# Float64 weights converted in five instructions on two engines, with the state loads split by batch

## The chip, the cores and the metric

The kernel runs on one NeuronCore of a Trainium2 chip. The metric is the device time of one execution in microseconds. The core has a matrix engine (TensorE, PE in the profile; its weight loads are PEld), a vector engine (VectorE, DVE), an engine for activation functions (ScalarE, ACT), GpSimd (POOL), which here only builds the identity matrix, and SyncE (SP), which issues the DMAs. Each engine works through its own instructions in order; they wait for each other through semaphores.

## The reference

x has 8 batches, 8 heads, 512 rows and 64 columns; state has 32 rows in place of the 512. An attention runs in both directions between them, and both results go through a two-layer block with the activation h * erf(softplus(h)):

```python
scores = scale * np.matmul(x, state.transpose(0, 1, 3, 2))
a = np.exp(scores - scores.max(-1, keepdims=True)); a /= a.sum(-1, keepdims=True) + 1e-09
xread = np.matmul(a, state)
scores2 = scale * np.matmul(state, x.transpose(0, 1, 3, 2))
a2 = np.exp(scores2 - scores2.max(-1, keepdims=True)); a2 /= a2.sum(-1, keepdims=True) + 1e-09
sread = np.matmul(a2, x)
x = concat([xread, sread], axis=2) as (B*(S+Ns), H*D)     # 4352 x 512
h = x @ w_in                                              # w_in 512 x 2048
g = h * erf(np.maximum(h, 0.0) + np.log1p(np.exp(-np.abs(h))))
out = g @ w_out                                           # w_out 2048 x 512
```

The two weights are the product of a float32 array and a float64 scalar and arrive as float64. Everything else is float32.

## The kernel before

**Chunks and units.** The output is made in nine chunks: chunk b for b = 0 to 7 holds the 512 rows of x of batch b, and chunk 8 the 256 state rows of all batches together. d_ff is cut into four groups g of 512 columns. One pass (b, g) is called a unit here. In a unit `hidden` (L237) makes the group's activations, `project` (L254) multiplies them by the group's part of w_out and adds them up over g in four PSUM banks. `project` is kept back by one unit (`pending`, L303 to L311): project of unit (b, g) stands in the program behind hidden of the next unit. After the last group `store` writes the chunk out.

**Mixed weights.** For chunks 0 to 7, xread is never made. `mixed(b, g)` (L224) multiplies the batch's states, transposed in `states(b)` (L132), by the group's columns of w_in, and `hidden` multiplies the attention weights aT by that. Chunk 8 uses w_in itself with sT, the results of the states' half.

**Attention.** `attention(b)` (L139) transposes x (L145), makes the scores (L155) and copies them to sc (L159). From there go two halves. The x half transposes the scores back (L170), takes maximum, difference, exponential, sum and quotient per head (L173 to L188) and transposes the result into aT (L199, L201). The states' half takes its own maximum (L178) and exponential (L181), transposes a2 (L193, L195), multiplies by x (L212) and puts the result into sT (L219, L220). hidden(b, 0) needs aT[b]; sT is not needed before chunk 8.

**Weights.** `weight` (L81) brings in one piece of 128 x 2 x 512 float64 (1 MB) through a raw buffer and makes it float32 in seven VectorE instructions: exponent (L96, L98, L99), sign (L100), mantissa (L103, L106) and their product (L108). The raw buffer has the tag hs and the intermediate the tag s, which are also the tags of hidden's own tiles; hs has two buffers, s three. A group has two pieces of w_in and two of w_out, 16 pieces in all, and they are loaded and converted in chunk 0, unit by unit (L295 to L298).

**Order.** The framework orders each engine's instructions itself, by program order as priority and by when it reckons an instruction to be ready, and lets a tile wait for a free buffer of its tag; what is quoted below is the order it made. In the program attention(0) comes first, then per unit of chunk 0: weights_in(g), mixed(0, g), weights_out(g), in unit 0 the loads of x for batch 1 and states(1), then hidden(0, g), the pending project, mixed(1, g), and in unit 1 attention(1). All DMAs are issued by SP: x of batch 0 (L67, eight DMAs), the states of all batches (L75, eight DMAs, one a head), then the weights (L90).

Of the kernel before, what the change touches and what calls it, by code (L numbers as in the profile page):

```python
# [8 lines left out]
F32 = mybir.dt.float32  # L9
# [7 lines left out]
def kernel(  # L17
# [51 lines left out]

    load_x(0)  # L70

    st = const.tile([P, B, P], F32, name="st")
    for h in range(H):
        i, e = h // 2, h % 2
        nc.sync.dma_start(out=st[Ns * i:Ns * i + Ns, :, D * e:D * e + D],  # L75
                          in_=state[:, h].rearrange("b n d -> n b d"))

    w_in = const.tile([P, NK, d_ff], F32, name="w_in")
    w_out = const.tile([P, NF, d_model], F32, name="w_out")

    def weight(dst, src, shape):  # L81


        if src.dtype == F32:
            nc.sync.dma_start(out=dst, in_=src)
            return
        i = shape[1]
        n = shape[0] * i
        raw = act.tile([P, 2 * n], U32, name="hs")
        nc.sync.dma_start(out=raw.rearrange("p (o i) -> p o i", i=2 * i), in_=src.bitcast(U32))  # L90
# [5 lines left out]
        nc.vector.tensor_scalar(e, hi, 20, 0x7FF, op0=ALU.logical_shift_right,  # L96
                                op1=ALU.bitwise_and)
        nc.vector.tensor_scalar(e, e, -896.0, 0.0, op0=ALU.add, op1=ALU.max)  # L98
        nc.vector.tensor_scalar(e, e, 255.0, 8388608.0, op0=ALU.min, op1=ALU.mult)  # L99
        nc.vector.scalar_tensor_tensor(out=e, in0=hi, scalar=0x80000000, in1=e,  # L100
                                       op0=ALU.bitwise_and, op1=ALU.bitwise_or)
# [4 lines left out]
        nc.vector.scalar_tensor_tensor(out=f, in0=lo, scalar=2.0 ** -32, in1=m,  # L106
                                       op0=ALU.mult, op1=ALU.add)
        nc.vector.scalar_tensor_tensor(  # L108
            out=dst, in0=f.rearrange("p (o i) -> p o i", i=i), scalar=2.0 ** -20,
            in1=e.bitcast(F32).rearrange("p (o i) -> p o i", i=i), op0=ALU.mult, op1=ALU.mult)  # L110
# [3 lines left out]
    def weights_in(g):  # L114
        fs = slice(gw * g, gw * g + gw)
        for k in range(0, NK, 2):
            weight(w_in[:, k:k + 2, fs],
                   moe_w_in[P * k:P * k + 2 * P, fs].rearrange("(k p) f -> p k f", p=P),
                   (2, gw))

    def weights_out(g):
        for t in range(GF * g, GF * g + GF, 2):
            weight(w_out[:, t:t + 2, :],
                   moe_w_out[P * t:P * t + 2 * P].rearrange("(t p) e -> p t e", p=P),
                   (2, d_model))
# [13 lines left out]
    def attention(b):  # L139
        xt = x_t.pop(b)  # L140
# [21 lines left out]
        a2 = att.tile([P, 2, S], F32, name="a2")  # L162
        a2T = att.tile([P, 2, NC, P], F32, name="a2T")
        aT[b] = keep.tile([P, 2, S], F32, name="aT")
        z2 = small.tile([P, 2], F32, name="z2")
        for e in range(2):

            s1 = ps_at.tile([P, NC * NI, Ns], F32, name="at")
            for c in range(NC):
                nc.tensor.transpose(out=s1[:, NI * c:NI * c + NI, :],  # L170
                                    in_=sc[:, e, P * c:P * c + P], identity=ident)
            m1 = small.tile([P, NC * NI], F32, name="m1")
            nc.vector.reduce_max(out=m1, in_=s1, axis=AX.X)  # L173
            nc.vector.tensor_tensor(a[:, e], s1, m1.unsqueeze(2).to_broadcast([P, NC * NI, Ns]),
                                    op=ALU.subtract)

            m2 = small.tile([P, 1], F32, name="m2")
            nc.vector.reduce_max(out=m2, in_=sc[:, e], axis=AX.X)  # L178
            nc.vector.tensor_scalar(m2, m2, -scale, None, op0=ALU.mult)
            nc.scalar.activation(out=a[:, e], in_=a[:, e], func=ACTF.Exp, scale=scale)  # L180
            nc.scalar.activation(out=a2[:, e], in_=sc[:, e], func=ACTF.Exp, bias=m2, scale=scale,  # L181
                                 accum_out=z2[:, e:e + 1])
            z1 = small.tile([P, NC * NI], F32, name="z1")
            nc.vector.reduce_sum(out=z1, in_=a[:, e], axis=AX.X)
            nc.vector.tensor_scalar(z1, z1, 1e-9, None, op0=ALU.add)
            nc.vector.reciprocal(z1, z1)
            nc.vector.tensor_tensor(a[:, e], a[:, e],
                                    z1.unsqueeze(2).to_broadcast([P, NC * NI, Ns]), op=ALU.mult)  # L188

        for e in range(2):  # L190
            ps = ps_at.tile([P, NC, P], F32, name="at")
            for c in range(NC):
                nc.tensor.transpose(out=ps[:, c, :], in_=a2[:, e, P * c:P * c + P],  # L193
                                    identity=ident)
            nc.scalar.copy(a2T[:, e], ps)  # L195
        for e in range(2):
# [5 lines left out]

        nc.vector.tensor_scalar(z2, z2, 1e-9, None, op0=ALU.add)
        nc.vector.reciprocal(z2, z2)
        sr = ps_at.tile([P, 2, D], F32, name="at")
        for e in range(2):
            for c in range(NC):
                for i in range(NI):  # L210
                    q = slice(Ns * i, Ns * i + Ns)
                    nc.tensor.matmul(out=sr[q, e, :], lhsT=a2T[:, e, c, q],  # L212
                                     rhs=xt[:, c, 2 * i + e, :],
                                     start=(c == 0), stop=(c == NC - 1))
        sn = small.tile([P, 2, D], F32, name="sn")
        for e in range(2):
            nc.vector.tensor_scalar(sn[:, e], sr[:, e], z2[:, e:e + 1], None, op0=ALU.mult)
        ps = ps_at.tile([P, NI, Ns], F32, name="at")
        nc.tensor.transpose(out=ps, in_=sn, identity=ident)  # L219
        nc.scalar.copy(sT[:, :, b, :], ps)  # L220
# [3 lines left out]
    def mixed(b, g):  # L224
# [3 lines left out]
        for i in range(NI):  # L228
            for e in range(2):
                r, q = slice(D * e, D * e + D), slice(Ns * i, Ns * i + Ns)  # L230
                nc.tensor.matmul(out=ps[e][q, :], lhsT=stT[b][r, q],  # L231
                                 rhs=w_in[r, i, gw * g:gw * g + gw], start=True, stop=True)
# [48 lines left out]
    def pairs(b, g):  # L281
# [3 lines left out]
        return [(w_in[:, k, gw * g:gw * g + gw], sT[:, k].rearrange("p b n -> p (b n)"))  # L285
# [61 lines left out]
```

## Time and profile before

| what | value |
|---|---|
| device time, median of 3 runs | 894.59 us (893.84 to 894.81) |
| device time of the profiled execution | 890.89 us |
| its span | 889.1 us |
| TensorE busy | 835.7 us (94%) |
| VectorE busy | 354.9 us (40%) |
| ScalarE busy | 351.7 us (40%) |
| mean granted TensorE clock | 0.979 |
| DMA | 35.09 MB, 39 GB/s over the span |

The span runs from the first to the last record of the core; the device time of the same execution is 1.8 us longer. The profile page divides the span into 40 slices of 22 us, with the busy share of each engine in tenths; its windows give the busy time of the engines between any two moments. A row of the timeline has the start and the length in us, the engine, the line of the kernel, the operation, the tile written and the tiles read, the shapes, the number of instructions that were merged, and in brackets the idle time before with what ended it. A row of a group ends with the busy time, the mean of one instruction in ns, and the idle time before. float32 matmuls appear as two records each; their ends are modelled, so that a busy TensorE isn't always one at full rate.

### The profile page before, as it was taken

The numbers are of one execution on the slowest core, as the hardware profiler recorded it, in microseconds if no ns is written. First come the engines' busy times: TensorE is split into PE (matmuls) and PEld (weight loads), VectorE is DVE, ScalarE is ACT, GpSimd is POOL, SyncE is SP. The second block draws the span as 40 slices with busy tenths as digits, with TensorE's granted clock in tenths as the row PEclk, the third lists the DMA queues.
The fourth block names the chain that finished last, engine by engine and source line by source line (L and its number), as shares of the span: only waits on it lengthen the run. The fifth ranks groups of instructions, "written<-read, shape, count | busy, mean of one in ns | idle before, by whom it ended". The sixth has DMA issues, their size and how long they took to land.

```text
span 889.1 us, 7809 instructions
## 1 busy us (share of the span) xinstructions
PE 835.7 (94%) x3216; PEld 378.6 (43%) x3216; DVE 354.9 (40%) x500; ACT 351.7 (40%) x460; POOL 0.7 (0%) x6
## 2 busy tenths in 40 slices
PE   3659859999999999999999999999999999999997
PEld 1314413344444444445444544444444444445664
DVE  3888998524322252226222522244222522222121
ACT  2221531535334453436343733444344534333342
POOL 0000000000000000000000000000000000000000
PEclk9579998999999999999999999999999999999999
DMA  8533254010201020102000020100010001000100
GB/s 212 142 128 109 96 141 142 1 48 0 49 0 48 0 49 0 48 0 48 1 24 24 1 48 0 48 0 1 0 48 0 2 0 39 9 0 1 47 1 24
DMA packets 45347, 35.09 MB, mean 39 GB/s; under 512 B 36865, under 2 KB 36865, under 8 KB 45313
## 3 DMA queue, kind: packets, MB, share of 16 engines
q1 hardware_dynamic: 45312, 34.61, 12.9%
q8 instruction: 25, 0.41, 0.2%
q14 instruction: 10, 0.07, 0.0%
HBM read 25.69 MB, written 8.91 MB: 39 GB/s over the span
## 4 chain that ended last, share of the span: by engine, by line
PE 83%; DVE 11%; DMA 3%; SPq 1%; ACT 1%; issue 0%; DVEq 0%
PE o L257 49%; PE h L246 26%; PE at L231 3%; DMA hs<-in_moe_w_in_dram 3%; DVE s L106 2%; DVE s L100 2%; PE at L145 1%; DVE s L96 1%; DVE s L103 1%; DVE s L98 1%; PE at L212 1%; PE at L155 1%; PE at L199 1%; PE at L193 1%; DVE w_in L108 1%; DVE s L251 1%
## 5 line engine op out<-in xcount | busy, mean ns | idle before, releaser
L257 PE MATMUL o<-w_out,s 128*128 128x512 f32 x1088 | 488.8, 597 | 15.1 <-DVE s L251 15.1
L257 PEld LDWEIGHTS o<-w_out,s 128*128 128x128 f32 x1088 | 204.0, 191 | 260.9 <-issue 241.7
L246 PE MATMUL h<-aT,m 128*128 128x512 f32 x512 | 240.4, 606 | 6.5 <-DVE hs L249 6.5
L249 DVE COPY hs<-h 128x512 f32<-128x512 f32 (+1 forms) x144 | 95.0, 660 | 245.5 <-ACT s L248 245.5
L248 ACT ACTIVATE s<-h 128x512 f32<-128x512 f32 (+1 forms) x144 | 82.2, 574 | 185.3 <-PE h L246 184.9
L246 PEld LDWEIGHTS h<-aT,m 128*128 128x128 f32 x512 | 93.9, 192 | 131.2 <-issue 116.9
L251 DVE TENSOR_TENSOR s<-s,hs 128x2048 f32<-128x2048 f32 (+1 forms) x36 | 78.2, 2173 | 74.7 <-ACT s L250 74.7
L233 ACT COPY m<-at 128x512 f32<-128x512 f32 x32 | 18.7, 585 | 210.0 <-PE at L231 210.0
L234 DVE COPY m<-at 128x512 f32<-128x512 f32 x32 | 22.1, 689 | 166.4 <-PE at L231 166.4
L250 ACT ACTIVATE s<-s 128x2048 f32<-128x2048 f32 (+1 forms) x36 | 65.4, 1815 | 0.4
L248 ACT ACT_TABLE_LOAD x42 | 53.9, 1283 | 14.2 <-DVE w_out L108 13.5
L231 PE MATMUL at<-w_in,stT 64*32 64x512 f32 x512 | 43.2, 629 | 4.0 <-DVE w_in L108 3.7
L250 ACT ACT_TABLE_LOAD x36 | 46.2, 1283 | 0.6
L265 ACT COPY ot<-o 128x512 f32<-128x512 f32 x34 | 19.8, 581 | 65.1 <-PE o L257 65.1
L246 PE MATMUL h<-sT,w_in 128*128 128x256 f32 x128 | 28.9, 379 | 0.0
L246 PEld LDWEIGHTS h<-sT,w_in 128*128 128x128 f32 x128 | 24.3, 190 | 6.7 <-issue 3.8
L231 PEld LDWEIGHTS at<-w_in,stT 64*32 64x32 f32 x512 | 6.8, 106 | 33.7 <-issue 22.9
L145 PE MATMUL at<-ident,x 128*128 128x128 f32 x128 | 18.3, 292 | 2.5 <-DVE m L234 2.2
L145 PEld LDWEIGHTS at<-ident,x 128*128 128x128 f32 x128 | 16.1, 151 | 10.4 <-DVE m L234 3.1
L147 ACT COPY xT<-at 128x512 f32<-128x512 f32 x32 | 17.4, 590 | 7.3 <-PE at L145 7.3
L96 DVE TENSOR_SCALAR s<-hs 128x1024 uint32<-128x1024 uint32 x16 | 11.0, 688 | 22.7 <-DMA hs<-in_moe_w_in_dram 22.7
L106 DVE SCALAR_TENSOR_TENSOR s<-hs,s 128x1024 f32<-128x1024 uint32 x16 | 19.5, 1218 | 0.1
(47 smaller groups left out, 295.8 us busy)
## 6 DMA issues: line engine op xcount, KB each, us to landing
x<-in_x_dram SPq DMA_DIRECT2D x64, 128.0 KB, 3.0
hs<-in_moe_w_in_dram SPq DMA_DIRECT2D x8, 1024.0 KB, 5.2
hs<-in_moe_w_out_dram SPq DMA_DIRECT2D x8, 1024.0 KB, 6.0
out_dram<-ot SPq DMA_DIRECT2D x32, 256.0 KB, 2.3
st<-in_state_dram SPq DMA_DIRECT2D x8, 64.0 KB, 2.3
out_dram<-ot SPq DMA_DIRECT2D x8, 64.0 KB, 1.7
```

Source lines behind the costliest of these rows:

```text
L96: nc.vector.tensor_scalar(e, hi, 20, 0x7FF, op0=ALU.logical_shift_right, op1=ALU.bitwise_and)
L106: nc.vector.scalar_tensor_tensor(out=f, in0=lo, scalar=2.0 ** -32, in1=m, op0=ALU.mult, op1=ALU.add)
L145: nc.tensor.transpose(out=xp[:, P * c:P * c + P], in_=xt[:, c, 2 * i:2 * i + 2, :], identity=ident)
L231: nc.tensor.matmul(out=ps[e][q, :], lhsT=stT[b][r, q], rhs=w_in[r, i, gw * g:gw * g + gw], start=True, stop=True)
L234: nc.vector.tensor_copy(mg[:, 1], ps[1])
L246: nc.tensor.matmul(out=hp[:, 0:n], lhsT=lhsT[:, P * i:P * i + P], rhs=rhs, start=(k == 0), stop=(k == len(pairs) - 1))
L248: nc.scalar.activation(out=s[:, i, :], in_=hp[:, 0:n], func=ACTF.Softplus)
L249: nc.vector.tensor_copy(hs[:, i, :], hp[:, 0:n])
L250: nc.scalar.activation(out=s, in_=s, func=ACTF.Erf)
L251: nc.vector.tensor_tensor(s, s, hs, op=ALU.mult)
L257: nc.tensor.matmul(out=acc[r], lhsT=gT[:, i, P * r:P * r + P], rhs=w_out[:, GF * g + i, :], start=(g == 0 and i == 0), stop=(g == NG - 1 a ...
L265: nc.scalar.copy(ot, acc[r])
```

## The change

Four things are changed.

- **The conversion** of a piece has two ScalarE and three VectorE instructions. ScalarE scales the high word, read as float32, into the destination, and scales the low word in place; VectorE shifts the destination by three bits, adds the low word, and puts in the sign. The intermediate in the s buffers is gone. w_in pieces get a raw tag of their own with two buffers; w_out pieces stay in hs. w_in is laid out by group, so that a piece is contiguous.
- **The states** of batch 0 are loaded first, from ScalarE's queue; those of the other batches from SP in unit 1 of chunk 0, behind that unit's weights.
- **Attention 0** is split: `attention` returns its states' half as a function, which is called behind hidden(0, 0). For later batches it is called at once; m2 and the a2 exponential then stand behind the whole x half.
- **Batch 1 comes later**: its x and states in unit 1, mixed(1, 0) and mixed(1, 1) both in unit 1, attention(1) in unit 3 of chunk 0. Later chunks keep their places.

```diff
+    def load_st(queue, bs):
+        for h in range(H):
+            i, e = h // 2, h % 2
+            queue.dma_start(out=st[Ns * i:Ns * i + Ns, bs, D * e:D * e + D],
+                            in_=state[bs, h].rearrange("b n d -> n b d"))
+
+    load_st(nc.scalar, slice(0, 1))
     load_x(0)
...
-    w_in = const.tile([P, NK, d_ff], F32, name="w_in")
+    w_in = const.tile([P, NG, NK, GF * P], F32, name="w_in")
...
-        raw = act.tile([P, 2 * n], U32, name="hs")
+        raw = act.tile([P, 2 * shape[0] * i], U32, name=tag, bufs=bufs)
...
-        em = act.tile([P, 2, n], U32, name="s", bufs=3)
-        e, m = em[:, 0], em[:, 1]
-        nc.vector.tensor_scalar(e, hi, 20, 0x7FF, op0=ALU.logical_shift_right,
-                                op1=ALU.bitwise_and)
-        nc.vector.tensor_scalar(e, e, -896.0, 0.0, op0=ALU.add, op1=ALU.max)
-        nc.vector.tensor_scalar(e, e, 255.0, 8388608.0, op0=ALU.min, op1=ALU.mult)
-        nc.vector.scalar_tensor_tensor(out=e, in0=hi, scalar=0x80000000, in1=e,
+        dst = dst.rearrange("p o i -> p (o i)")
+        d = dst.bitcast(U32)
+        nc.scalar.activation(out=dst, in_=hi.bitcast(F32), func=ACTF.Copy, scale=2.0 ** -112)
+        nc.scalar.activation(out=lo, in_=lo, func=ACTF.Copy, scale=2.0 ** -29)
+        nc.vector.tensor_scalar(d, d, 3, None, op0=ALU.logical_shift_left)
+        nc.vector.tensor_tensor(d, d, lo, op=ALU.add)
+        nc.vector.scalar_tensor_tensor(out=d, in0=hi, scalar=0x80000000, in1=d,
                                        op0=ALU.bitwise_and, op1=ALU.bitwise_or)
-
-        nc.vector.tensor_scalar(m, hi, 0xFFFFF, 0x100000, op0=ALU.bitwise_and,
-                                op1=ALU.bitwise_or)
-        f = m.bitcast(F32)
-        nc.vector.scalar_tensor_tensor(out=f, in0=lo, scalar=2.0 ** -32, in1=m,
-                                       op0=ALU.mult, op1=ALU.add)
-        nc.vector.scalar_tensor_tensor(
-            out=dst, in0=f.rearrange("p (o i) -> p o i", i=i), scalar=2.0 ** -20,
-            in1=e.bitcast(F32).rearrange("p (o i) -> p o i", i=i), op0=ALU.mult, op1=ALU.mult)
...
-    attention(0)
+    rest = attention(0)
...
+                if g == 1:
+                    load_st(nc.sync, slice(1, B))
-            if b + 1 < B and g == 0:
+            if b + 1 < B and g == (1 if b == 0 else 0):
                 load_x(b + 1)
                 states(b + 1)
             gT = hidden(pairs(b, g), n)
+            if b == 0 and g == 0:
+                rest()
...
-            if b + 1 < B:
-                mixed(b + 1, g)
-                if g == 1:
-                    attention(b + 1)
+            if b + 1 < B and (b or g):
+                for i in [g] if b or g > 1 else [0, 1]:
+                    mixed(b + 1, i)
+                if g == (NG - 1 if b == 0 else 1):
+                    attention(b + 1)()
```

More of the change, by code (lines that the diff above doesn't have):

```diff
@@ L116, in weights_in @@
         for k in range(0, NK, 2):
-            weight(w_in[:, k:k + 2, fs],
+            weight(w_in[:, g, k:k + 2, :],
                    moe_w_in[P * k:P * k + 2 * P, fs].rearrange("(k p) f -> p k f", p=P),
-                   (2, gw))
+                   (2, gw), "raw", 2)
     def weights_out(g):
@@ L190, in attention @@
         for e in range(2):
[L191 to L196, printed above, removed]
             ps = ps_at.tile([P, S], F32, name="at")
@@ L201, in attention @@
             nc.vector.tensor_copy(aT[b][:, e], ps)
[L205 to L214, printed above, removed]
@@ L222 @@
+        return rest
     m_t = {}
```

61 lines of the change are left out of this document (37 added, 24 removed).

## The prediction

> **What bounds the kernel now.** I read the page's busy shares in 40 slices first, to see where TensorE is not the limit, then its windows by stage.
>
> ```profile
> span 889.1 us, 7809 instructions
> ...
> PE   3659859999999999999999999999999999999997
> ...
> DVE  3888998524322252226222522244222522222121
> ```
>
> ```profile
> 12.48:40.56 28.08, 17.50 (x140) 9.61 (x140) 22.86 (x41) 8.49 (x17) 0.00 (x0) 0.69 0.71 202
> 40.56:170.00 129.44, 103.55 (x422) 40.47 (x422) 113.02 (x147) 42.67 (x57) 0.00 (x0) 0.92 0.34 109
> 170.00:889.10 719.10, 714.64 (x2657) 328.51 (x2655) 219.00 (x314) 299.25 (x385) 0.00 (x0) 1.00 0.06 19
> ```
>
> The columns of a window are its length, then PE, PEld, DVE, ACT and POOL busy, the granted clock, the DMA share and GB/s. After 170 us TensorE is busy for all but the tail, at clock 1.00: nothing there is to be won or, short of a new stall, lost. Before 170 VectorE is busy 22.86 + 113.02 = 135.9 of 157.5 us, and TensorE waits and runs at 0.69 and 0.92. So the opening is bound by VectorE and by what waits for it.
>
> How much could be won follows from the work of TensorE. The chain of waits and the timeline, of one mixed and of TensorE's end, give it:
>
> ```profile
> 245.92 12.02 PE o L257 x28
> ...
> 308.08 1.24 PE at L155 x16
> ...
> 402.93 1.24 PE at L155 x16
> ```
>
> ```profile
> 119.17 1.09 PE L231 MATMUL at<-w_in,stT 64*32 64x512 f32 x16
> ```
>
> ```profile
> 836.29 3.62 PE L246 MATMUL h<-sT,w_in 128*128 128x256 f32 x16
> 839.74 1.02 PE L257 MATMUL o<-w_out,s 128*128 128x512 f32 x2
> ...
> 871.60 13.04 PE L257 MATMUL o<-w_out,s 128*128 128x512 f32 x30
> ```
>
> A matmul record at full clock takes 12.02/28 = 0.43 us, and the same place of two attentions is 402.93 - 308.08 = 94.85 us apart: one batch with everything in it (4 hidden of 16 records, 6.9 us each; 4 project of 32, 13.7 us; 4 mixed at 1.09; one attention, the rest, about 8). The last chunk is 8 x 3.45 (839.74 - 836.29) + 64 x 0.43 = 55.1. So all matmul work is 8 x 94.85 + 55.1 = 813.9 us. It starts at 12.48; the last matmul ends at 871.60 + 13.04 = 884.64, 4.5 before the end. 12.48 + 813.9 + 4.5 = 830.9: **58.2 us of the span are lost**, all before 170.
>
> Where they are lost, from the timeline of the opening:
>
> ```profile
> 0.73 5.36 SPq L67 DMA_DIRECT2D x<-in_x_dram  x8
> 6.14 4.07 SPq L75 DMA_DIRECT2D st<-in_state_dram  x8
> 10.25 0.96 SPq L90 DMA_DIRECT2D hs<-in_moe_w_in_dram  x2
> 12.48 0.45 PE L135 MATMUL at<-ident,st 128*128 128x128 f32 x1 [12.48 <-DMA st<-in_state_dram]
> 15.43 0.69 DVE L96 TENSOR_SCALAR s<-hs 128x1024 uint32<-128x1024 uint32 x1 [15.43 <-DMA hs<-in_moe_w_in_dram]
> 16.64 0.69 DVE L98 TENSOR_SCALAR s<-s 128x1024 uint32<-128x1024 uint32 x1
> 17.25 1.22 DVE L106 SCALAR_TENSOR_TENSOR s<-hs,s 128x1024 f32<-128x1024 uint32 x1
> 18.21 1.07 ACT L159 COPY sc<-at 128x512 f32<-128x512 f32 x2 [1.22 <-PE at L155]
> 18.38 0.68 DVE L99 TENSOR_SCALAR s<-s 128x1024 uint32<-128x1024 uint32 x1
> ...
> 30.03 0.69 DVE L201 COPY aT<-at 128x512 f32<-128x512 f32 x1
> ...
> 36.40 1.22 DVE L108 SCALAR_TENSOR_TENSOR w_in<-s 128x1024 f32<-128x1024 f32 x1
> ...
> 40.56 5.06 PE L246 MATMUL h<-aT,m 128*128 128x512 f32 x8
> ```
>
> The first matmul waits for the state, which SP issues behind x. attention(0) is through at 30.7, but the first w_in group only at 37.6, so the first hidden starts at 40.56. By then 9.1 us of matmul work (attention 8, mixed 1.1) are done in 28.1: **19.0 lost; the other 39.2 follow**. Who makes them wait, from the waits between 40.56 and 170:
>
> ```profile
> PE o L257 <- DVE s L251: 15.1, 3, 7.4
> ...
> ACT L248 <- DVE w_out L108: 13.5, 3, 5.0
> ...
> DVE s L96 <- DMA hs<-in_moe_w_in_dram: 7.3, 4, 2.3
> PE h L246 <- DVE hs L249: 6.5, 2, 3.3
> ```
>
> ```profile
> SPq L90 <- DVE s L100: 36.5, 7, 6.9
> SPq L90 <- DVE s L251: 23.1, 3, 10.8
> ```
>
> Each row has the sum, the times and the longest. The fourth is VectorE waiting for weights; the other three of the first group are in-order delays behind the conversion, and the s buffers that it holds. The last two, from SP's own waits, are weight loads that wait for an hs buffer, those on L251 until a whole hidden is finished.
>
> **The conversion.** Two forms are in it: the one-source operations (L96, L98, L99, L103) follow each other at 17.25 - 16.64 = 0.60 us, those with two sources (L100, L106, L108) at 18.38 - 17.25 = 1.13. Before: 4 x 0.60 + 3 x 1.13 = 5.8 a piece, 16 pieces, 93 us. After: one shift 0.60, an addition and a bitwise operation of two sources, 2 x 1.13: 2.9 a piece, 46 us. **VectorE loses 47 us** and comes to 89 in an opening whose matmul work is longer.
>
> ```profile
> L251 DVE TENSOR_TENSOR s<-s,hs 128x2048 f32<-128x2048 f32 x4 | 9.1, 2284 | 2.5 <-ACT s L250 2.5
> ```
>
> The addition of two uint32 tensors is in no row; its bounds are 0.60 (a one-source operation of that size) and 2.28 (L251, two sources and twice the size), and I take 1.13, the row of the same size with two tensor sources.
>
> ScalarE gets two operations of 128x1024 a piece. Their nearest rows in the opening are half and double:
>
> ```profile
> L248 ACT ACTIVATE s<-h 128x512 f32<-128x512 f32 x18 | 10.3, 596 | 26.9 <-PE h L246 26.9
> L250 ACT ACTIVATE s<-s 128x2048 f32<-128x2048 f32 x4 | 7.6, 1911 | 0.0
> ```
>
> Between 0.60 and 1.91, on their line, lies 0.60 + 1.31/3 = 1.03. 32 of them are **33 us on ScalarE**, which had 8.49 + 42.67 = 51.2 us of work in 157.5; bounds 32 x 0.60 = 19 and 32 x 1.91 = 61. 51 + 33 = 84 fits under the opening even if that shrinks by 58, so I cost it at nothing for the bound, but not for the latency: each piece passes two engines, about 1.0 + 1.0 + 1.1 + 1.1 = 4.2 us from landing to the end. What is queued behind a ScalarE operation that waits for a weight DMA is attention's copies and exponentials and hidden's softplus, and TensorE waits for all of them.
>
> **The loads.** Eight state issues (4.07 us) leave SP's head, so the weights go out at about 6.1 instead of 10.25. On ScalarE's queue eight issues cost between nothing and, at SP's rate, 4.07 us, before its table load; x lands later than that, so nothing. The page gives x 3.0 us from issue to landing:
>
> ```profile
> x<-in_x_dram SPq DMA_DIRECT2D x64, 128.0 KB, 3.0
> ```
>
> The last x is out at 6.1 and lands at 9.1: TensorE starts **3.4 us earlier**. The other seven batches' states (again eight issues, some 4.1 us) and x of batch 1 (5.4) go on SP, with the loads of the second and third groups behind them; these have at least 21 us of hidden and project work as cover. Without that cover they would cost their 9.5 us. The raw buffers of w_in take away the 23.1 us of loads that wait for L251, and the s buffers no longer go to the conversion (the 13.5 us of ScalarE).
>
> **The first hidden.** sc was copied 18.21 - 12.48 = 5.7 us after the first matmul, aT ready 12.5 later, at 30.7, with conversion operations between and the states' half as well. From 9.1 the same makes 27.3. VectorE by itself: the first piece lands 5.2 after its issue (15.43 - 10.25), at 11.3, so it starts around 12.8, and has ten operations of attention at 0.60, about 0.8 of small ones, two pieces (5.7) and mixed's copy: 13.1 us, to 25.9. I take **27 for the first hidden**: 13.6 earlier.
>
> **The sum.** From there: 813.9 - 9.1 and the states' half of attention 0, moved behind it. Its TensorE part is in these rows of attention 1 (the first of them twice): 2 x 0.66 + 1.10 + 0.27 = 2.7.
>
> ```profile
> 92.06 1.09 PE L145 MATMUL at<-ident,x 128*128 128x128 f32 x8 [2.21 <-DVE m L234]
> ...
> 103.57 0.66 PE L193 MATMUL at<-ident,a 128*128 128x128 f32 x4 [0.23 <-ACT a L181]
> ...
> 107.25 1.28 DVE L201 COPY aT<-at 128x512 f32<-128x512 f32 x2
> ...
> 108.47 1.10 PE L212 MATMUL at<-x,a2T 128*32 128x64 f32 x64
> ...
> 112.18 0.27 PE L219 MATMUL at<-ident,sn 128*128 128x128 f32 x1
> ```
>
> 27 + 804.8 + 2.7 + 4.5 = 839.0 without another loss. Losses that I leave in, my estimates: 3.4 because half of the first hidden still runs at the half clock (16 x 0.43 / 2; the clock was 0.69 in the window before it); 3 because VectorE owes two w_out pieces, two w_in pieces, the hidden copies and L251, some 16 us from 27, where TensorE has 13; 2 a unit for the three later units, 6; 2.6 around attention 1. That is 15: a span of **854**, 35 less. The profiled execution took 890.89 with 1.8 outside the span, so 856; the timed runs have a median of 894.59, 3.7 above the profiled one, and 894.6 - 35 gives **860**. Its own range is 850 to 867.
>
> **The rivals.** *ScalarE's order.* It is in order, and a conversion placed ahead of attention's copies waits for its DMA: VectorE already waited up to 2.3 us for the w_in loads, 7.3 in four waits. Four groups at 3 us or so more are 12 us: 872. For: two more engines' hand-overs a piece; against: ScalarE has much idle time. In sentences of its own: the Trainium skill, ScalarE: Activation LUTs, section Rules for kernel authors, has multiplications done on VectorE, not ScalarE, as up to about three times as fast there in bf16. The trace agrees in direction for float32 (0.69 against an estimated 1.03), and that trade is this rival; it decides only where ScalarE is late.
>
> *attention 1 exposed.* It moves from the second unit to the end of chunk 0. In the rows above it took 92.06 to 108.5 to aT, 16.5 us of which 5.3 (8 less 2.7) are its own matmuls; if nothing fills it, 11 us: 871. Against: project of the last two units, 27.5 us, is ready about then. In sentences of its own: the Trainium skill, TensorE: Matmul & The Clock Gate, section What's actually happening, gives half clock after an idle window of about 3.4 us; by it the exposed case would cost up to 1.7 more, an estimate from that page. The trace shows the half clock after idling (0.69 above).
>
> *Better*: the losses left in are 5, and the first hidden starts at 25: 848.
>
> *Slower than before*: the strided uint32 reads and integer writes of ScalarE are in no row. If they ran far slower than the float rows, ScalarE would bound the opening. It has 157.5 - 51.2 = 106 us free at the old length, so from 106/32 = 3.3 us each, over three times my value, the change loses; at 4 us it gives 894.6 + 32 x 0.7 = 917. Nothing in the profile points there.
>
> That the conversion path isn't taken is excluded: the loads through hs are in the trace.
>
> **Chances.** Forecast 0.50, ScalarE's order 0.20, attention exposed 0.14, better 0.09, slower 0.04, gain given back to within 0.2% (what a measurement can tell) 0.03. So faster 0.93, same 0.03, slower 0.04. 847 to 878 takes in all but the last two and the worst of the rivals.
>
> **What would show it.** Right: the first hidden before 30, VectorE some 47 us less busy, ScalarE some 33 more, the first matmul near 9, weight loads no longer waiting for L251, the distance between attentions still 94.85. Wrong: conversions of ScalarE near 2 us or more; ScalarE idle on weight DMAs ahead of softplus; TensorE idle for over 5 us between the last hidden of chunk 0 and the first of chunk 1; any TensorE gap in the later chunks.

## The result and the profile after

The changed kernel takes 855.66 us (median of 4 runs, 854.35 to 856.09) against 894.70 us for the kernel before on the same chip (4 runs, 893.84 to 896.83): a ratio of 0.9558, 95% interval 0.9538 to 0.9578. It is 39.0 us faster. The profiled execution took 856.09 us, 1.8 more than its span.

The page of the changed kernel: span, busy time of each engine, and the 40 slices (21.4 us each) of TensorE, VectorE, ScalarE and TensorE's clock.

```profile
span 854.3 us, 7812 instructions
...
PE 827.7 (97%) x3216; PEld 379.0 (44%) x3216; DVE 310.8 (36%) x436; ACT 388.9 (46%) x494; POOL 0.7 (0%) x6
...
PE   3689999999999999999999999999999999999997
...
DVE  2979524452222522262224422262224322222121
ACT  5778535563344534373344534373445434333332
...
PEclk7689999999999999999999999999999999999999
```

Before, TensorE reached nine tenths for good only in the seventh slice; now it does so in the fourth. VectorE is 44.1 us less busy (354.9 before), ScalarE 37.2 more (351.7 before). The windows of the changed kernel, cut at its first matmul, at its first hidden and at 130 us; the columns are those of the windows in the prediction:

```profile
6.59:32.52 25.93, 13.44 (x66) 6.65 (x66) 16.55 (x25) 15.73 (x20) 0.00 (x0) 0.62 0.78 269
32.52:130.00 97.48, 94.68 (x386) 38.16 (x386) 64.10 (x74) 62.75 (x72) 0.00 (x0) 0.94 0.43 132
130.00:854.30 724.30, 719.59 (x2767) 334.14 (x2765) 230.13 (x338) 309.18 (x402) 0.00 (x0) 1.00 0.07 20
```

In the opening the clock column (0.62 and 0.94 here) is only an upper bound: the lengths of TensorE's matmuls show it slower in places than the column does (last section). The middle row is where the time came from. Before, from the first hidden to 170 us TensorE was idle for 129.44 - 103.55 = 25.9 us at a clock of 0.92. Now it is idle for 97.48 - 94.68 = 2.8 us at 0.94. With the prediction's account (813.9 us of matmul work at full clock, 4.5 of tail), the span of 854.3 is 6.6 to the first matmul, 6.4 of matmul work (9.1 less the states' half, 2.7) and 19.5 lost before the first hidden, 807.5 of work after it, 9.8 lost there, and the tail. Of the 9.8, 2.8 are the idle time and about 94.68 x 0.06 = 5.7 the lower clock, an estimate from that row; the rest, 1.3, is not assigned. The matmuls bear out most of that: the first eight records of the hidden at 32.52 and of the next, at 49.93, take 5.75 and 5.50 us, where the second eight at 38.92 take 3.70, 3.9 us in all. So 29.3 us are lost after the first matmul where 58.2 were before, and the start is 5.9 earlier; together that is the 34.8 by which the span is shorter.

The groups of the changed kernel between 5 and 135 us: the new conversion of w_in, two ScalarE and three VectorE instructions a piece.

```profile
L103 DVE CUSTOM_DVE_ANT_0 w_in<-raw,w_in 128x2048 uint16<-128x2048 uint16 x8 | 9.8, 1219 | 0.9 <-ACT raw L101 0.8
L104 DVE SCALAR_TENSOR_TENSOR w_in<-raw,w_in 128x1024 uint32<-128x1024 uint32 x8 | 9.7, 1211 | 0.1
L101 ACT ACTIVATE raw<-raw 128x1024 uint32<-128x1024 uint32 x8 | 9.2, 1156 | 0.0
L100 ACT ACTIVATE w_in<-raw 128x1024 f32<-128x1024 f32 x8 | 9.2, 1152 | 8.8 <-DMA raw<-in_moe_w_in_dram 8.8
L102 DVE TENSOR_SCALAR w_in<-w_in 128x1024 uint32<-128x1024 uint32 x8 | 5.4, 686 | 14.1 <-ACT w_in L100 14.1
```

The addition of two uint32 tensors takes 1.22 us, as long as the bitwise operation with two sources of the same size. ScalarE takes 1.15 to 1.16 us for each of its two. And SP's own waits of the changed kernel (sum, times, longest):

```profile
SPq L95 <- DVE w_out L104: 27.8, 4, 10.1
SPq L95 <- DVE w_in L104: 20.0, 4, 9.3
SPq L95 <- DVE s L249: 7.7, 2, 5.5
```

The loads that wait for a whole hidden (L249 now, L251 before) went from 23.1 us to 7.7; the rest waits for a raw buffer that is being converted.

Last, the timeline of the opening, from the first DMA to the first hidden:

```profile
0.74 4.34 ACTq L76 DMA_DIRECT2D st<-in_state_dram  x8
...
6.59 0.45 PE L130 MATMUL at<-ident,st 128*128 128x128 f32 x1 [6.59 <-DMA st<-in_state_dram]
...
7.19 1.13 SPq L95 DMA_DIRECT2D raw<-in_moe_w_in_dram  x2
...
12.91 1.12 ACT L100 ACTIVATE w_in<-raw 128x1024 f32<-128x1024 f32 x1 [2.70 <-DMA raw<-in_moe_w_in_dram]
13.93 0.58 ACT L143 COPY xT<-at 128x512 f32<-128x512 f32 x1
...
14.56 1.94 PE L151 MATMUL at<-xT,stT 64*32 64x512 f32 x10 [2.47 <-ACT xT L143]
...
16.56 1.08 ACT L155 COPY sc<-at 128x512 f32<-128x512 f32 x2 [1.01 <-PE at L151]
...
26.14 1.09 PE L179 MATMUL at<-ident,a 128*128 128x128 f32 x4 [6.98 <-DVE a L173]
...
28.99 2.81 PE L229 MATMUL at<-w_in,stT 64*32 64x512 f32 x16
...
29.10 0.69 DVE L181 COPY aT<-at 128x512 f32<-128x512 f32 x1
...
32.52 5.75 PE L244 MATMUL h<-aT,m 128*128 128x512 f32 x8 [0.72 <-ACT m L231]
```

The first matmul starts at 6.59 instead of 12.48. But ScalarE then takes up the first piece's scaling (L100) ahead of the fourth copy of x (L143) and waits 2.70 us for the piece's DMA; the copy ends at 14.5, and TensorE waits 2.47 for it. At the end, mixed (L229) stands behind the transposes of attention 0, so that the first hidden follows aT (29.79) by 2.7. It takes 2.81 us there, at clock 0.50 and with a wait of 0.68 for the copy of aT in it, where the prediction's row of a mixed has 1.09.

### The profile page after: what moved, and what is told of

The parts are those of the page before. It is cut to its first block, busy times and chain, and to the rows that moved or that the text cites. A ratio compares the mean times of both kernels' runs of the same rounds, so it can differ in the third digit from the quotient of the medians.

```text
span 854.3 us, 7812 instructions
## 1 busy us (share of the span) xinstructions
PE 827.7 (97%) x3216; PEld 379.0 (44%) x3216; DVE 310.8 (36%) x436; ACT 388.9 (46%) x494; POOL 0.7 (0%) x6
## 4 chain that ended last, share of the span: by engine, by line
PE 91%; DVE 0%; ACT 0%; issue 0%
PE o L255 53%; PE h L244 28%; PE at L229 4%; PE at L141 1%; PE at L151 1%; PE at L208 1%; PE at L196 1%; PE at L179 1%; PE at L162 1%; PE at L215 0%; PE at L130 0%; DVE m L232 0%; ACT ot L263 0%
## 5 line engine op out<-in xcount | busy, mean ns | idle before, releaser
L249 DVE TENSOR_TENSOR s<-s,hs 128x2048 f32<-128x2048 f32 (+1 forms) x36 | 78.3, 2174 | 74.0 <-ACT s L248 74.0
L229 PE MATMUL at<-w_in,stT 64*32 64x512 f32 x512 | 40.6, 628 | 0.4 <-DVE m L232 0.4
L143 ACT COPY xT<-at 128x512 f32<-128x512 f32 x32 | 17.3, 589 | 7.8 <-PE at L141 7.8
L229 PEld LDWEIGHTS at<-w_in,stT 64*32 64x32 f32 x512 | 6.4, 106 | 27.0 <-issue 20.8
L179 PE MATMUL at<-ident,a 128*128 128x128 f32 x64 | 9.4, 292 | 7.7 <-DVE a L173 7.7
L151 PE MATMUL at<-xT,stT 64*32 64x512 f32 x128 | 11.9, 637 | 2.5 <-ACT xT L143 2.5
```

The lines of the kernel that those rows point to most:

```text
L151: nc.tensor.matmul(out=s2[e][q, :], lhsT=stT[b][r, q], rhs=xT[r, i, :], start=True, stop=True)
L229: nc.tensor.matmul(out=ps[e][q, :], lhsT=stT[b][r, q], rhs=w_in[r, g, i, :], start=True, stop=True)
L249: nc.vector.tensor_tensor(s, s, hs, op=ALU.mult)
```

## The experiments

All kernels differ from the changed kernel by the edit shown, except e6, which starts from the kernel before. None of them leaves out work. Times are medians; the changed kernel's 855.7 is the mark. The starts of the first and third hidden, (0, 0) and (0, 2), are from the timelines; the kernels that are 9 us or more slower than the changed one are those whose third hidden starts at 90 us or later. The start is no measure of the loss by itself: e4 and e6 have the attention of batch 1 ahead of their third hidden, and e1, which has not, starts it earlier than both and is slower.

| kernel | us | ratio to before, 95% interval | span | first hidden | third hidden |
|---|---|---|---|---|---|
| kernel before | 894.70 | 1 | 889.1 | 40.56 | 114.79 |
| changed kernel | 855.66 | 0.9558, 0.9538 to 0.9578 | 854.3 | 32.52 | 81.13 |
| e1 old conversion | 881.5 | 0.9849, 0.9812 to 0.9886 | 878.8 | 34.81 | 99.06 |
| e6 new conversion alone | 876.56 | 0.9799, 0.9784 to 0.9814 | 874.6 | 36.59 | 105.61 |
| e2 w_in shares hs | 865.1 | 0.9663, 0.9628 to 0.9698 | 863.7 | 32.38 | 90.44 |
| e4 order of before | 866.45 | 0.9681, 0.9639 to 0.9724 | 864.2 | 36.31 | 105.12 |
| e5 no split of attention 0 | 856.13 | 0.9566, 0.9540 to 0.9592 | 855.1 | 37.87 | 83.07 |
| e3 states on SP | 857.35 | 0.9575, 0.9537 to 0.9613 | 854.2 | 35.93 | 81.21 |
| e7 weights first | 856.18 | 0.9581, 0.9563 to 0.9600 | 853.3 | 34.52 | 78.84 |
| e9 scaling on VectorE | 857.78 | 0.9592, 0.9575 to 0.9608 | 857.8 | 30.52 | 84.20 |
| e10 extra matmuls | 858.45 | 0.9596, 0.9581 to 0.9611 | 857.6 | 34.24 | 84.81 |
| e11 other order | 855.57 | 0.9557, 0.9531 to 0.9584 | 854.2 | 32.83 | 81.45 |
| e12 e11 with weights first | 856.46 | 0.9563, 0.9536 to 0.9590 | 855.6 | 33.85 | 83.67 |
| e13 e11 with w_in loads ahead | 857.48 | 0.9573, 0.9545 to 0.9602 | 855.9 | 32.65 | 81.80 |

### Which part of the change carries the gain

**e1_old_conv**: the seven VectorE instructions back, with the s buffers as their intermediate; all else as changed.

```diff
-        nc.scalar.activation(out=dst, in_=hi.bitcast(F32), func=ACTF.Copy, scale=2.0 ** -112)
-        nc.scalar.activation(out=lo, in_=lo, func=ACTF.Copy, scale=2.0 ** -29)
...
+        em = act.tile([P, 2, n], U32, name="s", bufs=3)
...
+        nc.vector.tensor_scalar(e, hi, 20, 0x7FF, op0=ALU.logical_shift_right,
+                                op1=ALU.bitwise_and)
...
```

> The changed kernel with the seven-instruction VectorE conversion put back (its intermediate again in the s buffers); buffers of w_in, state loads and order as changed. Theory A (the conversion's VectorE time is most of the gain): VectorE again has some 44 us more in the opening and bounds it, 880 to 890 us. Rival B (the loads' own buffers and the order are most of it): 860 to 868 us, with VectorE fuller but TensorE hardly idle.

Measured 881.5: 25.8 us of the 39 are lost without the new conversion. The windows of e1 show VectorE as the bound again after the first hidden:

```profile
6.00:35.00 29.00, 13.27 (x66) 6.27 (x67) 20.78 (x33) 6.04 (x12) 0.00 (x0) 0.69 0.75 248
35.00:100.00 65.00, 53.70 (x219) 20.87 (x220) 61.22 (x79) 22.61 (x29) 0.00 (x0) 0.85 0.55 163
```

VectorE is busy for 61.22 of 65 us, and TensorE for 53.70. e1 puts back two things at once, VectorE's work and the s buffers that the old conversion holds; no run parts them.

**e6_conv_alone**: the kernel before with the new conversion and the layout of w_in that it needs; buffers, states and order stay as they were.

```diff
-    w_in = const.tile([P, NK, d_ff], F32, name="w_in")
+    w_in = const.tile([P, NG, NK, GF * P], F32, name="w_in")
...
-        em = act.tile([P, 2, n], U32, name="s", bufs=3)
...
+        nc.scalar.activation(out=dst, in_=hi.bitcast(F32), func=ACTF.Copy, scale=2.0 ** -112)
+        nc.scalar.activation(out=lo, in_=lo, func=ACTF.Copy, scale=2.0 ** -29)
...
```

> The kernel before with only the five-instruction conversion (and w_in laid out by group, which its addition needs); all loads, buffers and the order as before. Theory A (the conversion's VectorE time is most, and what is left needs the s buffers freed, which this also does): 868 to 874 us. Rival B (without buffers and order the loads bound the opening instead): 878 us or more.

Measured 876.56, between the two expectations: alone, the conversion gives 18 us. A row of its waits of TensorE says where the rest is held up:

```profile
PE o L248 <- DVE s L242: 14.1, 3, 6.9
```

project still waits 14.1 us for the end of hidden, which before had been 15.1 (on L251). So the new conversion needs the other parts to give its whole gain, and they need it: taken away one by one from the changed kernel, conversion, raw buffers (9.4, e2) and order (10.8, e4) cost 46 us together, more than the 39 there are.

**e2_shared_hs**: w_in pieces in hs again.

```diff
-                   (2, gw), "raw", 2)
+                   (2, gw), "hs", 2)
```

> The changed kernel with the w_in pieces back in the two hs buffers. Theory A: loads wait for hidden again, but with a short conversion that costs one load and one conversion per group at most: 857 to 864 us. Rival B (buffers are most of the gain): 872 us or more.

Measured 865.1, one microsecond above the first theory's range: the raw buffers are worth 9.4 us. In e2's waits the row of the kernel before is back, if smaller:

```profile
PE o L255 <- DVE s L249: 6.6, 3, 3.9
```

**e4_old_order**: attention 0 whole, and batch 1's x, states, mixed and attention in the units where they were before.

```diff
-    rest = attention(0)
+    attention(0)()
...
-            if b + 1 < B and g == (1 if b == 0 else 0):
+            if b + 1 < B and g == 0:
...
-            if b + 1 < B and (b or g):
-                for i in [g] if b or g > 1 else [0, 1]:
-                    mixed(b + 1, i)
-                if g == (NG - 1 if b == 0 else 1):
+            if b + 1 < B:
+                mixed(b + 1, g)
+                if g == 1:
```

> The changed kernel with attention 0 whole ahead of the weights, and batch 1's loads, states, mixed and attention back in the first two units. Theory A: the states' half is again among the work ahead of the first hidden, on VectorE and TensorE, and attention 1 fills VectorE while it has conversions to do: 858 to 864 us. Rival (the order is worth nothing, or attention 1 at the end of the chunk was costing time): 851 to 856 us.

Measured 866.45: 10.8 us, somewhat more than expected. In its waits project stands 6.3 us at once on L249. e4 undoes two things; the next kernel divides them.

**e5_no_split**: attention 0 whole, batch 1 late as changed.

```diff
-    rest = attention(0)
+    attention(0)()
...
-            if b == 0 and g == 0:
-                rest()
```

> The changed kernel with attention 0 whole again ahead of the weights; batch 1 stays late. It parts the 11 us of e4_old_order between its two edits. Theory A2 (batch 1's work in the first units is what costs, because it takes VectorE and ScalarE while they have conversions): 856 to 858 us here. Rival (the states' half ahead of the first hidden is what costs): 861 us or more.

Measured 856.13, which can't be told from the changed kernel. The first hidden starts 5.4 us later, at 37.87, and nothing of it is left at the end. So, by difference, e4's 10.8 us come from where batch 1's work stands, and no worth of the split of attention 0 shows here.

**e3_states_sp**: all states on SP behind x, as before.

```diff
-    load_st(nc.scalar, slice(0, 1))
     load_x(0)
+    load_st(nc.sync, slice(0, B))
...
-                if g == 1:
-                    load_st(nc.sync, slice(1, B))
```

> The changed kernel with all states loaded on SP behind x of batch 0, as before. Theory A: first matmul 5 to 6 us later, first weights on SP 4 us later, both on the path to the first hidden: 859 to 861 us. Rival: the first hidden waits for VectorE's queue and not for the start, so 855 to 857 us.

Measured 857.35, and a span of 854.2, that of the changed kernel: within half a microsecond of the rival's range and below the first theory's. Two rows of its timeline:

```profile
12.39 0.44 PE L130 MATMUL at<-ident,st 128*128 128x128 f32 x1 [12.39 <-DMA st<-in_state_dram]
...
35.93 3.70 PE L244 MATMUL h<-aT,m 128*128 128x512 f32 x8 [0.96 <-ACT m L231]
```

TensorE starts 5.8 us later than in the changed kernel and the first hidden 3.4, but its eight records take 3.70 us, where the changed kernel's first eight take 5.75, the first of them at half the clock. So no gain of the states' own queue shows. It isn't excluded either: the median is 1.7 us above the changed kernel's, the four executions run from 855.61 to 858.69, and the profiled one is among the shorter.

### What holds the first hidden, and what an earlier one is worth

**e7_weights_first**: the first two w_in loads on SP ahead of x, to take ScalarE's wait of 2.70 us away.

```diff
-    load_st(nc.scalar, slice(0, 1))
-    load_x(0)
...
+    first = weights_in(0)
+    load_st(nc.scalar, slice(0, 1))
+    load_x(0)
     states(0)
```

> The changed kernel with the first two w_in loads issued on SP ahead of x of batch 0; their conversion keeps its place in the program. Theory: ScalarE's in-order wait for these loads ahead of attention's copies (2.7 us) goes, and VectorE starts some 5 us earlier: first hidden 3 to 6 us earlier, 850 to 853 us. Rival C (an earlier first hidden runs at the half clock, so nothing is won): 854 to 857 us. If x comes so late that attention waits for it: 857 us or more.

Measured 856.18, which can't be told from the changed kernel. From its timeline:

```profile
8.96 0.69 DVE L103 TENSOR_SCALAR w_in<-w_in 128x1024 uint32<-128x1024 uint32 x1 [8.96 <-ACT w_in L101]
9.79 0.45 PE L129 MATMUL at<-ident,st 128*128 128x128 f32 x1 [9.79 <-DMA x<-in_x_dram]
...
27.77 1.09 PE L178 MATMUL at<-ident,a 128*128 128x128 f32 x4 [6.97 <-DVE a L172]
...
34.52 4.97 PE L243 MATMUL h<-aT,m 128*128 128x512 f32 x8
```

VectorE starts 5.1 us sooner and ScalarE no longer waits, but x comes later, and the attention with it: the first hidden is 2.0 later. The wait was exchanged for another. The time is in rival C's range for another reason than C's: the first hidden came later and not earlier. The third case, in which attention waits for x, is what happened, 0.8 us below the 857 given for it.

**e9_scale_dve**: both scalings on VectorE.

```diff
-        nc.scalar.activation(out=dst, in_=hi.bitcast(F32), func=ACTF.Copy, scale=2.0 ** -112)
-        nc.scalar.activation(out=lo, in_=lo, func=ACTF.Copy, scale=2.0 ** -29)
+        nc.vector.tensor_scalar(dst, hi.bitcast(F32), 2.0 ** -112, None, op0=ALU.mult)
+        nc.vector.tensor_scalar(lo, lo, 2.0 ** -29, None, op0=ALU.mult)
```

> The changed kernel with the two scalings of a piece on VectorE as one-source operations and none on ScalarE. VectorE gets 32 x 0.60 = 19 us more, ScalarE loses 37. Theory A (VectorE bounds the stretch to the second hidden): 6 to 10 us slower, 861 to 866 us. Rival D (ScalarE's order is what costs): equal or faster, 850 to 856 us.

Measured 857.78, 2 us slower, between the two theories. The windows of e9:

```profile
6.00:30.00 24.00, 12.79 (x65) 6.07 (x65) 15.98 (x27) 5.38 (x11) 0.00 (x0) 0.73 0.77 258
30.00:60.00 30.00, 20.10 (x117) 9.43 (x118) 28.53 (x41) 15.00 (x20) 0.00 (x0) 0.76 0.74 217
```

The first hidden comes 2.0 earlier (30.52), since nothing waits on ScalarE; then VectorE is busy for 28.53 of 30 us, and more than that is given back. Both engines can do the scaling, and in this kernel it hardly matters which.

**e10_warm**: ten matmuls of 128x512 into a bank that is overwritten later, placed in TensorE's idle time of attention 0, to keep its clock up.

```diff
+    x0 = x_t[0]
     rest = attention(0)
+    warm = ps_o.tile([P, d_model], F32, name="o3")
+    for j in range(10):
+        nc.tensor.matmul(out=warm, lhsT=ident, rhs=x0[:, j % NC, :, :], start=True, stop=True)
```

> The changed kernel with ten matmuls of 128x512 in TensorE's idle time around attention 0, into a PSUM bank that nothing reads before the first project overwrites it. Theory C (the first hidden loses some 3 us to the half clock): clock 0.9 or more between 25 and 45 us and 851 to 853 us. Rival (the half clock costs nothing there, since VectorE's queue sets the pace): 854 to 857 us.

Measured 858.45, 3 us slower; both expectations missed. Its windows:

```profile
20.00:30.00 10.00, 6.38 (x22) 2.95 (x20) 10.00 (x18) 8.15 (x9) 0.00 (x0) 0.98 0.57 170
30.00:40.00 10.00, 9.93 (x27) 3.60 (x28) 8.29 (x13) 4.98 (x7) 0.00 (x0) 0.51 0.48 101
```

The clock was held between 20 and 30 us and had fallen when the first hidden ran (at 34.24). So what a full clock in the first hidden is worth isn't known from this run.

### What holds the later part

e3, e5, e7, e9 and e10 move the first hidden between 30.5 and 37.9 us, and the time moves by 3. In all of them the third hidden starts between 79 and 85 us. Three kernels try to move that.

**e11_order**: the first group's w_out goes through the s buffers and is converted behind the second group's w_in; the states' half of attention 0 is called in the second unit.

```diff
-                weights_in(g)
-                mixed(0, g)
-                weights_out(g)
+            if b == 0 and g == 0:
+                for c in first:
+                    c()
+                mixed(0, 0)
+                out0 = weights_out(0, "s", 3)
+            elif b == 0:
+                for c in weights_in(g):
+                    c()
+                mixed(0, g)
+                for c in (out0 if g == 1 else []) + weights_out(g):
+                    c()
...
-            if b == 0 and g == 0:
+            if b == 0 and g == 1:
                 rest()
```

> The changed kernel with another order in the opening: the first w_out group waits in s buffers and is converted behind the second w_in group, and the states' half of attention 0 comes behind the second hidden. Theory E (the second hidden at 50 us, and not the first, is what the opening waits for: it waits for the second w_in group, and in TensorE's order for the states' half): second hidden at 42 to 46 us and 848 to 852 us. Rival (the total is set by VectorE's whole queue, so that another order only moves the wait): 854 to 857 us.

Measured 855.57: the rival's number. The second hidden starts 3.1 us earlier (46.80 for 49.93), the third at 81.45, and nothing is won.

**e12_first_order**: e11's order with e7's loads.

> e11_order with the first two w_in loads ahead of x as in e7_weights_first. Theory E: now the earlier start of VectorE reaches the second hidden, 1 to 4 us below e11_order. Rival C (what starts earlier runs at the half clock): the same as e11_order.

Measured 856.46: the rival's time again, but not its mechanism. The first hidden starts 1.0 us later than in e11, not earlier, and the third at 83.67.

**e13_order_next**: e11, and on SP the next group's w_in ahead of this group's w_out.

```diff
                 mixed(0, 0)
+                first = weights_in(1)
                 out0 = weights_out(0, "s", 3)
...
-                for c in weights_in(g):
+                for c in first:
                     c()
                 mixed(0, g)
+                if g + 1 < NG:
+                    first = weights_in(g + 1)
```

> The kernel of e11_order with one more thing moved: on SP the loads of the next group's w_in stand ahead of this group's w_out loads, so that the third w_in group no longer stands behind the hs load that waits for the end of hidden(0, 0) at 50 us. Nothing is left out. Theory F (that load is what holds the third hidden at 81 to 84 us in every variant, whatever the first and second do): the w_in loads of the third group go out by 48, the third hidden starts at 70 to 78, and what e11_order won at the second hidden (3.1 us) and the gaps behind it stay won: 849 to 853 us. Rival G (TensorE's own backlog of project and attention work, and ScalarE's order, set the third hidden): the loads go out earlier but the third hidden stays at 80 to 84, and the time at 854 to 857.

Measured 857.48, half a microsecond above the range of rival G, with the third hidden where G has it. Theory F falls. In the changed kernel both loads of the third w_in group went out at 50.44, behind a w_out load that had waited for hidden (0, 0). In e13 they went out at 34.60 and 41.43, but the second of these pieces was converted no earlier. e11's timeline, then e13's:

```profile
67.58 1.16 ACT L101 ACTIVATE w_in<-raw 128x1024 f32<-128x1024 f32 x1
...
72.32 1.22 DVE L105 SCALAR_TENSOR_TENSOR w_in<-raw,w_in 128x1024 uint32<-128x1024 uint32 x1
...
81.45 3.70 PE L243 MATMUL h<-aT,m 128*128 128x512 f32 x8 [0.18 <-ACT m L230]
```

```profile
41.43 0.37 SPq L93 DMA_DIRECT2D raw<-in_moe_w_in_dram  x1
42.30 1.14 ACT L101 ACTIVATE w_in<-raw 128x1024 f32<-128x1024 f32 x1
...
67.61 1.15 ACT L101 ACTIVATE w_in<-raw 128x1024 f32<-128x1024 f32 x1
...
72.52 1.22 DVE L105 SCALAR_TENSOR_TENSOR w_in<-raw,w_in 128x1024 uint32<-128x1024 uint32 x1
...
81.80 3.70 PE L243 MATMUL h<-aT,m 128*128 128x512 f32 x8
```

The high word of the first piece is scaled at 42.30, that of the second only at 67.61, 26 us after its load went out, in e11 at 67.58. The window from 50 to 70 us, of e13:

```profile
50.00:70.00 20.00, 19.46 (x112) 8.95 (x111) 15.98 (x19) 19.88 (x24) 0.00 (x0) 0.97 0.58 187
```

ScalarE is busy for 19.88 of 20 us there (19.88 in e11 too). Four of its instructions in that window are table loads (ACT_TABLE_LOAD) of 1.28 us, 5.1 us together, in front of softplus, of erf and of the exponential of the states' half. What follows, as a reading of these windows: with the loads out of the way, the third group is kept by when the converting engines come to it, in e11 and e13 ScalarE. Taking the scalings off ScalarE doesn't help: in e9 it is busy for 7.42 us of the same 20, but VectorE for 19.30, and the third hidden starts at 84.20. And TensorE is busy for 19.46 of 20 in e13: past 50 us there is next to nothing left to win, whichever wait is taken away. None of the twelve kernels is faster than the changed one by more than its interval.

## Why the prediction was right, point by point

**The bound** (the opening, by VectorE and what waits for it): right. e1 shows it: with the old conversion back, VectorE is the bound between 35 and 100 us and two thirds of the gain are gone. One reading of its rows is off: in the first group of waits the third row, not the fourth, is VectorE waiting for weights.

**The conversion**: right, VectorE is 44.1 us less busy where 47 was forecast, and the addition that no row had shown costs what the row with two tensor sources costs (1.22 busy, the same as L104). That the time fell by nearly as much isn't a proof of one for one: e6 gives 18 us alone, e1 takes away 26.

**ScalarE**: mechanism right, size a little low: 1.15 to 1.16 for 1.03, 37.2 us for 33. It was costed at nothing for the bound. That held in the changed kernel (62.75 of 97.48 us), but with less room than the sum over the opening says: between 40 and 50 us ScalarE was busy for 9.93 of 10, and in e11 and e13 for 19.88 of 20. In those ten microseconds three table loads take 3.8 us; up to 130 us there are 11 of them, 8 in the kernel before, and the prediction didn't count them. The prediction's own rival of scaling on ScalarE against VectorE is decided by e9, narrowly: 2 us slower on VectorE, with intervals that just overlap. In a sentence of its own: the rule of the Trainium skill, ScalarE: Activation LUTs, section Rules for kernel authors, to multiply on VectorE holds for the single instruction here (0.68 in e9's group of L100 against 1.15) and not for the kernel, whose VectorE has the less room.

**The loads**: the start was underestimated. TensorE starts 5.9 us earlier, not 3.4: the prediction took x's landing as the end of the wait, but the first matmul needs the states alone, which land first. The weights, though, went out later than forecast, at 7.19 and not 6.1, because the issues of x took 6.41 us where they had taken 5.36. e3 shows no gain of the earlier start at the end. The 23.1 us of waits on L251 fell to 7.7, not to none; hs is still shared by w_out's pieces. e2 gives the raw buffers 9.4 us.

**The first hidden** is the step that was mis-sized: forecast 27, measured 32.52. Its parts stand in the timeline above. First, the copy of sc was forecast for 9.1 + 5.7 = 14.8 and starts at 16.56: TensorE was 2.5 early, but from the first matmul to sc it took 9.97 and not 5.7. In that stretch L100 stands ahead of the fourth copy of x on ScalarE and waits 2.70 for its DMA. That is the rival "ScalarE's order", which cost TensorE time once, and not four times at 3 us: in all ScalarE waited 13.5 us for weight DMAs (8.8 for w_in, 4.7 for w_out, seven waits), but between 5 and 135 us TensorE's waits for ScalarE are 4.0 us, 2.5 of them this one. From sc to aT it took 13.2 (16.56 to 29.79) for the 12.5 taken. Second, the prediction let hidden follow aT at once, and mixed with its copies came last, 2.7 us more, of which 1.7 are mixed itself (2.81 for 1.09, by the low clock and the wait for aT's copy). 1.8, 0.7 and 2.7 are 5.2 of the 5.5; the last 0.3 lies between the 27.3 that this path gave and the 27 that was taken.

**The losses after it**: 9.8 where 15 were left in, 5.2 less. The parts were off by more than the sum. Of the 15, 11.6 were waits and 3.4 the clock; measured are 2.8 us of idle time and about 5.7 of clock. So the waits were 8.8 too many, the clock 2.3 too little, 1.3 are not assigned, and the first hidden was 5.5 late: 5.5 - 8.8 + 2.3 + 1.3 = 0.3. That the span agrees within 0.3 is luck. Why the errors offset each other in part can be seen in e3, e5, e7 and e9: the first hidden moved over 7 us and the span by under 5, and not in the same order. The prediction didn't foresee that.

**Attention 1 at the end of chunk 0**: right that it isn't exposed. The rival's gap of 5 us or more isn't there: TensorE is idle for only 2.8 us between 32.52 and 130, and behind 130, where attention 1 ends, for 724.30 - 719.59 = 4.7 us, all of it the tail. e4 says that the move was needed: in the old place the order costs 10.8 us. The prediction gave the order no gain of its own; its sum counts from TensorE's work and so takes the loss in the old place as gone without naming it.

**The steady state**: right, unchanged, with TensorE at clock 1.00.

**The number**: the span was 0.3 from its forecast; the timed median is 4.3 below 860, because the forecast carried the 3.7 us by which the timed runs of before lay above their profiled one, and the changed kernel's timed runs lie 0.4 below its own.

What stays open: whether an order written by hand, with fewer table loads in it, would win any of the 19.5 us before the first hidden and the 9.8 behind it; how much of e1's loss is VectorE's work and how much the s buffers; and what a full clock in the first hidden is worth.

## What to carry to other kernels

An engine that bounds a stage can be relieved by moving part of its work to one with room in that same stage, and the room is to be read in windows of 10 or 20 us: an engine with 51 us of work in 157 looked free, and yet there were stretches without room. When moved starts don't move the end (the first hidden by 7 us, the third by 6, the time by 3), look at TensorE's busy share behind them before taking away one wait more: at 2.8 us of idle time in 97 there was nothing left. And where an engine takes work in order, look for a step that waits for a DMA ahead of a short copy that others wait for (2.5 us of TensorE here); that moving it pays isn't shown, since e7 took this wait away and got another.

## What the runs showed of the hardware

The addition of two uint32 tensors appears in the trace as a custom operation on 128x2048 uint16, twice the elements of its operands, and takes 1.22 us, no longer than the two-source operation on 128x1024 uint32.

The clock column has to be held against the length of the matmuls. Windows and groups of transposes of the changed kernel:

```profile
28.00:36.00 8.00, 7.28 (x24) 2.56 (x25) 7.93 (x11) 5.37 (x6) 0.00 (x0) 0.50 0.63 167
...
L179 PE MATMUL at<-ident,a 128*128 128x128 f32 x8 | 2.2, 427 | 7.7 <-DVE a L173 7.7
...
L196 PE MATMUL at<-ident,a 128*128 128x128 f32 x8 | 1.2, 272 | 0.0
```

and of e7:

```profile
28.00:36.00 8.00, 6.83 (x27) 2.52 (x27) 7.66 (x14) 4.61 (x8) 0.00 (x0) 1.00 0.32 104
...
L178 PE MATMUL at<-ident,a 128*128 128x128 f32 x8 | 2.2, 427 | 7.2 <-DVE a L172 7.2
...
L195 PE MATMUL at<-ident,a 128*128 128x128 f32 x7 | 0.9, 272 | 0.0
```

The first group of each kernel is from 26 to 31 us, the second from 38 to 46. Both kernels wait 7 us for the quotient of attention 0 ahead of the first group (6.97 in e7's row above, 6.98 in the timeline of the changed kernel's opening). The column has 0.50 for the changed kernel and 1.00 for e7 there. But the same transposes take 427 ns on average in both, and in both only 272 ns later. So e7 was as slow as the changed kernel behind the gap, and its 1.00 isn't a full rate. The kernel before has the same at its start: its first transpose, at 12.48, takes 0.45 us with the column at 1.00, and a later one of the same size, at 112.18, takes 0.27 (both rows are in the prediction). A kernel's mean clock is no better for comparing executions: the changed kernel's four have 0.981, 0.995, 0.997 and 0.987 and lie within 1.7 us, the shortest not at the highest clock.

In sentences of its own: the Trainium skill, TensorE: Matmul & The Clock Gate, section What's actually happening, has the half clock after one idle window of about 3.4 us and the full one after a busy window of the same length. The lengths of the matmuls agree in direction: 427 ns among the waits of attention 0 and 272 ns from 38 us on, behind the first hidden. They show neither the length of the windows nor what this gap did, since eight transposes ahead of it already take 2.0 us in both kernels.
